# Windowed attention and a max-of-three FFN on one core: chunk 2's K and Q on GpSimd's queue, and a new order for the first five chunks

## The chip, the core and the metric

The kernel runs on one NeuronCore of a Trainium2 chip. A core has TensorE for matrix products (PE in the profile, its weight loads PEld), VectorE (DVE), ScalarE (ACT), GpSimd (POOL) and SyncE (SP), which here only starts transfers. GpSimd too starts transfers, on a queue of its own. Each engine works through its own instructions in program order and waits at each one until what it needs is there. The metric is the device time of one execution in microseconds, the median of several runs.

## The reference

Attention for 4 batches, 8 heads, 768 positions of 64 values: a query sees the 4 first keys of its batch (the sink) and the 128 latest keys up to itself. The result, 3072 tokens of 512 values, goes through an FFN with three weights of 512 x 768, of which the largest product is taken per element, and an output weight of 768 x 512.

```python
scores = scale * np.matmul(q, k.transpose(0, 1, 3, 2))
keep = is_sink | in_window              # pos < 4, or 0 <= rel < 128
a = softmax(np.where(keep, scores, -1e9))
x = np.matmul(a, v)                     # tokens x (heads * 64)
h = np.maximum(np.maximum(x @ w1, x @ w2), x @ w3)
return h @ w_out
```

All inputs and the output are float32; the kernel multiplies in bfloat16.

## The kernel before, in words

A chunk is 256 tokens of one batch with all 8 heads; there are 12, three per batch (`NCH`, `CPB`). Chunks 0 to 5 have one layout (`NEW = 6`), the later ones another. Heads go in four pairs p. Chunks 0, 3, 6 and 9 begin a batch and see no earlier keys.

The stages of a chunk ci, by helper:

- `load` (L93) starts a transfer of K, Q or V, whole (512 KB) or by halves of the heads (`part`), from SP's queue unless `eng` names another. A `gate` is a tiny GpSimd instruction that writes one element of the destination, so that the transfer waits for it: `pool_gate` (L605) waits for nothing but its place on GpSimd, `after(wi, c)` (L599) reads an element of FFN weight wi and so waits until the third of that weight with column c has landed. K, Q and V each have two buffers, so that chunk ci + 2 takes the one of chunk ci.
- `cast_qk` (L112) and `cast_v` (L121) turn float32 into bfloat16, a half of a chunk's Q or K, or a quarter of its V, on the engine that the call names.
- `turn` (L132), `turn2` (L156) and `turn_dma` (L177) transpose Q and K: the first two by TensorE with a copy from the accumulator memory (PSUM) by the engine named, the last by a transfer from SP.
- `premask` (L306) puts a pair's mask into its score banks ahead of the scores, by two matmuls of 512 columns (384 in a chunk that begins a batch). A pair without it is masked after the exponential by a VectorE multiply, `mask` (L401). `score` (L314) multiplies, `expo` (L392) takes the exponential on ScalarE, two instructions per pair.
- `sink_k` (L278), `sink_score` (L408) and `sink_v` (L431) do the four sink keys.
- `av_open` (L445) takes four PSUM banks, one per pair, and adds the sink's part; `av` (L460) multiplies a pair's weights by V, and VectorE divides by the sum: a reciprocal (L476) and a multiply (L479).
- `xpose` (L485) transposes the result x by TensorE, with two copies; `xpose_dma` (L496) by a transfer.
- `ffn_h` (L504): nine calls per chunk, third fp of the columns by weight wi, each of 8 matmuls with 256 columns (L517). The product with weight 0 is copied by ScalarE (L523), the others are merged by a maximum on VectorE (L527).
- `ffn_y` (L532): one of two halves of the tokens times the output weight, 6 matmuls of 512 columns (L540), and a copy. From chunk 3 on `y_turn` (L551, matmuls L564) does this. `store` (L591) writes a chunk's y from SP; `store_half` (L595) writes every second token row of it.

The weights come from GpSimd's queue, cast on the way: `load_w` (L289) nine times, a third of one weight each, and `load_wo` (L297) twice, half of the output weight.

PSUM has eight banks. `bank` hands out the one that has been free longest in the order of the program text, and `give` puts it back; so the text also sets which instruction waits for which bank.

The order of chunks 0 to 3, and of chunk 4 up to its FFN, is written out by hand, one helper call per line (L626 to L877). From L878 a loop handles iteration i: the attention of chunk i + 1, the FFN of chunk i, the output of chunk i - 1, the casts of chunk i + 2 on GpSimd and the loads of chunk i + 3. In the iterations i = 9 and i = 10 it also stores y of chunks 0 and 1 (one transfer of 1024 KB, both chunks lie in one tile) and of chunk 2.

In the written order, chunk 2's K (two halves) and Q (two halves) are started by SP (L697 to L704), gated by the second third of weight 0 and by GpSimd's place; chunk 2's V (L715) has the first gate too. GpSimd issues weight 2's thirds at L705 to L708, the output weight at L729. Chunk 1 has pairs 0 and 1 masked ahead of the scores and pairs 2 and 3 on VectorE; chunk 2 has all four on VectorE.

Of the kernel before, what the change touches and what calls it, by code (L numbers as in the profile page):

```python
# [16 lines left out]
def kernel(  # L17
# [31 lines left out]
    with tc.manual_schedule():  # L49
# [410 lines left out]
        def av(ci, p):  # L460
# [4 lines left out]
            for t in range(2):  # L465
                for a in range(2):
# [3 lines left out]
                    for s, cv, n in blocks:  # L470
# [3 lines left out]
                        first = False  # L474
            rc = work.tile([128, 2, 2], F32, tag="rc", bufs=4, name="rc")
# [9 lines left out]
        def xpose(ci, t, eng=None):  # L485
# [4 lines left out]
            for ds in range(DS):  # L490
                nc.tensor.transpose(
                    pt[:, ds], xs[ci][:, ds, t].rearrange("q a d -> q (a d)"), ident)
# [11 lines left out]
        def ffn_h(ci, fp, wi, cuts=1, eng=nc.scalar):  # L504
# [3 lines left out]
            for f in range(2):  # L508
                c0 = (2 * fp + f) * 128
                for ds in range(DS):  # L510
# [3 lines left out]
                    else:  # L514
# [5 lines left out]
                        start=(ds == 0), stop=(ds == DS - 1))  # L520
            dst = hs[ci][:, 2 * fp:2 * fp + 2]
# [103 lines left out]

        load(0, 'q', part=1, parts=2)  # L626
        warm(8)
        load(0, 'k')
        load(0, 'q', part=0, parts=2)
        load(0, 'v', part=0, parts=2, gate=pool_gate)  # L630
        cast_qk(0, 'q', 1, nc.scalar)
        load(0, 'v', part=1, parts=2)
        masks()
        sink_init()
        factors(msk, addm)
        turn(0, 'q', 1, nc.scalar)
        warm(4)
        premask(0, (2,))
        cast_qk(0, 'k', 0, nc.scalar)
        cast_qk(0, 'k', 1, nc.vector)  # L640
        turn(0, 'k', 1, nc.vector)
        load(1, 'k')
        turn(0, 'k', 0, nc.scalar)
        cast_qk(0, 'q', 0, nc.gpsimd)
        premask(0, (3,))
        score(0, (2,))
        score(0, (3,))
        turn(0, 'q', 0, nc.vector)
        premask(0, (0,))
        load(1, 'q')  # L650
        expo(0, 2)
        cast_v(0, 1, 0, nc.gpsimd)
        cast_v(0, 0, 0, nc.vector)
        cast_v(0, 1, 1, nc.vector)
        cast_v(0, 0, 1, nc.vector)
        load_w(0, 512, 768)
        load(1, 'v')
        score(0, (0,))
        expo(0, 3)
        cast_qk(1, 'k', 0, nc.gpsimd)  # L660
        premask(0, (1,))
        score(0, (1,))
        expo(0, 0)
        expo(0, 1)
        load_w(0, 256, 512)
# [3 lines left out]
        turn2(1, 'k', 0, nc.vector)  # L669
        cast_qk(1, 'k', 1, nc.scalar)  # L670
        av(0, 0)
        cast_qk(1, 'q', 0, nc.gpsimd)
        cast_qk(1, 'q', 1, nc.scalar)
        turn(1, 'k', 1, nc.scalar)
        load_w(0, 0, 256)
        av(0, 1)
        premask(1, (0,))
        turn2(1, 'q', 0, nc.vector)
        sink_k(0)
        premask(1, (1,))  # L680
        turn(1, 'q', 1, nc.scalar)
        cast_v(1, 0, 0, nc.vector)
        cast_v(1, 1, 0, nc.vector)
        load_w(1, 512, 768)
        xpose(0, 0, nc.vector)
        score(1, (0,))
        score(1, (1,))
# [190 lines left out]
        for i in range(4, NCH):  # L878
# [57 lines left out]
            if i == NCH - 2:  # L936
                store(2)
# [43 lines left out]
```

## Time and profile before

| what | us |
|---|---|
| three runs, median (lowest to highest) | 176.03 (175.41 to 176.61) |
| the profiled execution's own time | 175.3 |
| its span in the profile | 173.6 |
| TensorE busy | 167.1 |
| VectorE busy | 124.7 |
| GpSimd busy | 110.9 |
| ScalarE busy | 88.7 |

Times inside the profile count from the start of the span; 1.7 us of the profiled execution's time lie around it. "Busy" is the union of an engine's instruction times; TensorE's instructions overlap, so that it can count as busy while it delivers less than it could. The granted clock of TensorE was full throughout. A timeline row gives the start, the length, the engine, the line, the operation, its tile and shapes, how many, and in brackets how long the engine was idle before it and what ended that. A row of the chain of waits gives start, length, engine, tile, line and count. A row of stretches gives from:to, length, then busy time and number of instructions of TensorE, its weight loads, VectorE, ScalarE and GpSimd, the granted clock, the mean busy share of the DMA engines and GB/s. A row of one group of instructions gives the shortest, median and longest duration in ns.

### The profile page before, as it was taken

The page shows a single profiled execution, that of the slowest core. Times are in us where ns is not written, and L with a number is a line of the kernel's source. Part 1 is how long each engine was busy: PE and PEld are TensorE (multiplying, and loading weights), DVE is VectorE, ACT ScalarE, POOL GpSimd, SP SyncE. Part 2 cuts the span into 40 slices and gives each one's busy share as a digit, 9 for nine tenths or more (in the row PEclk, how much of TensorE's full clock was granted, in tenths as well). Part 3 has the DMA queues.
Part 4 walks back from the last instruction along what each step waited for, and adds up shares of the span by engine and source line. Part 5 has one row for each costly group of instructions (what it writes and reads, how often), then busy time and mean ns, then how long its engine had stood idle before and what let it go on. Part 6 is the DMA issues. An engine that isn't in the chain of part 4 may idle for free.

```text
span 173.6 us, 5416 instructions
## 1 busy us (share of the span) xinstructions
PE 167.1 (96%) x2225; PEld 128.6 (74%) x2225; DVE 124.7 (72%) x262; ACT 88.7 (51%) x183; POOL 110.9 (64%) x193
## 2 busy tenths in 40 slices
PE   7979999999999999999999999999999999999992
PEld 2546888857696697797797797797797896896871
DVE  3387854796797985986877976877777776776361
ACT  4778544677954614817726717717636516510210
POOL 7399507545499999999999999999998600000000
PEclk9999999999999999999999999999999999999999
DMA  4999999999999997988999999989999119017303
GB/s 139 301 288 198 218 217 256 221 306 276 280 195 216 190 273 124 245 199 216 253 199 252 195 224 246 265 168 227 264 195 259 32 33 377 21 34 272 121 2 121
DMA packets 71545, 35.22 MB, mean 203 GB/s; under 512 B 27488, under 2 KB 69984, under 8 KB 71520
## 3 DMA queue, kind: packets, MB, share of 16 engines
q1 hardware_dynamic: 65824, 31.60, 79.0%
q0 software_dynamic: 5552, 3.15, 12.7%
q8 instruction: 17, 0.28, 0.7%
q10 hardware_dynamic: 144, 0.13, 0.2%
q14 instruction: 8, 0.07, 0.1%
HBM read 25.17 MB, written 6.29 MB: 181 GB/s over the span
## 4 chain that ended last, share of the span: by engine, by line
PE 85%; DMA 7%; POOL 5%; issue 1%; DVE 0%; POOLq 0%; SPq 0%
PE h_ps L517 52%; PE y_ps L564 11%; PE y_ps L540 7%; PE o L471 6%; DMA w<-in_moe_w_dram 4%; PE st L357 3%; DMA v_raw<-in_v_dram 3%; PE st L331 2%; POOL w L292 2%; POOL vb L123 1%; PE pt L138 1%; PE o L453 1%; PE y_ps L586 1%; PE sk L423 1%; POOL q_bf L118 0%
## 5 line engine op out<-in xcount | busy, mean ns | idle before, releaser
L517 PE MATMUL h_ps<-xT,w 128*128 128x256 bf16 x864 | 101.2, 273 | 0.2 <-DMA w<-in_moe_w_dram 0.2
L517 PEld LDWEIGHTS <-w 128*128 128x128 bf16 x864 | 81.7, 98 | 10.7 <-issue 0.5
L527 DVE TENSOR_TENSOR h_sb<-h_sb,h_ps 128x512 bf16<-128x512 bf16 (+1 forms) x74 | 49.0, 670 | 17.4 <-PE h_ps L517 15.6
L523 ACT CAST h_sb<-h_ps 128x512 bf16<-128x512 f32 x35 | 20.6, 589 | 51.3 <-PE h_ps L517 51.2
L129 POOL CAST vb<-v_raw 32x512 bf16<-32x512 f32 x48 | 36.8, 766 | 2.5 <-DMA v_raw<-in_v_dram 0.3
L90 POOL CAST k_bf<-k_raw 32x512 bf16<-32x512 f32 x48 | 29.6, 616 | 2.2
L398 ACT ACTIVATE e_sb<-st 128x512 bf16<-128x512 f32 (+1 forms) x48 | 23.1, 583 | 1.1 <-PE st L331 1.1
L479 DVE TENSOR_TENSOR x_sb<-o,rc 128x256 bf16<-128x256 f32 x48 | 20.4, 424 | 1.7
L564 PE MATMUL y_ps<-wo,h_sb 64*64 64x512 bf16 (+1 forms) x312 | 21.1, 377 | 0.0
L471 PE MATMUL o<-vb,e_sb 128*128 128x65 bf16 x352 | 16.5, 193 | 0.8 <-DVE vb L123 0.8
L471 PEld LDWEIGHTS <-e_sb 128*128 128x128 bf16 x352 | 14.5, 97 | 3.1 <-ACT e_sb L398 1.0
L123 POOL CAST vb<-v_raw 64x512 bf16<-64x512 f32 x18 | 12.6, 697 | 5.7 <-DMA v_raw<-in_v_dram 5.1
L389 DVE TENSOR_TENSOR e_sb<-e_part,msk 128x1024 bf16<-128x1024 bf16 x16 | 13.1, 831 | 3.3 <-ACT e_part L374 3.1
L406 DVE TENSOR_TENSOR e_sb<-e_sb,msk 128x1024 bf16<-128x1024 bf16 (+1 forms) x18 | 13.6, 776 | 2.3 <-ACT e_sb L398 2.1
L564 PEld LDWEIGHTS <-h_sb 64*64 64x64 bf16 (+1 forms) x312 | 9.9, 106 | 5.0
L374 ACT ACTIVATE e_part<-st 128x384 bf16<-128x384 f32 x32 | 13.1, 495 | 0.5 <-PE st L357 0.5
L540 PE MATMUL y_ps<-wo,h_sb 128*128 128x512 bf16 x54 | 12.8, 380 | 0.0
L476 DVE RECIPROCAL rc<-o 128x4 f32<-128x4 f32 x48 | 8.4, 174 | 4.0 <-PE o L471 3.8
L118 POOL CAST k_bf<-k_raw 128x512 bf16<-128x512 f32 x6 | 3.8, 650 | 9.5 <-PE pt L138 6.8
L118 ACT CAST q_bf<-q_raw 128x512 bf16<-128x512 f32 x13 | 7.6, 620 | 3.0 <-DMA q_raw<-in_q_dram 3.0
L540 PEld LDWEIGHTS <-h_sb 128*128 128x128 bf16 x54 | 4.8, 98 | 5.4 <-DVE h_sb L527 0.8
L427 ACT ACTIVATE e_sink<-sk 128x256 bf16<-128x256 f32 x8 | 3.1, 389 | 10.0 <-PE sk L423 10.0
(90 smaller groups left out, 142.9 us busy)
## 6 DMA issues: line engine op xcount, KB each, us to landing
k_raw<-in_k_dram SPq DMA_DIRECT2D x11, 512.0 KB, 5.6
v_raw<-in_v_dram SPq DMA_DIRECT2D x11, 512.0 KB, 5.6
q_raw<-in_q_dram SPq DMA_DIRECT2D x10, 512.0 KB, 6.9
out_dram<-y_sb SPq DMA_DIRECT2D x9, 512.0 KB, 3.1
w<-in_moe_w_dram POOLq DMA_DIRECT2D x9, 256.0 KB, 6.1
q_raw<-in_q_dram SPq DMA_DIRECT2D x4, 256.0 KB, 7.6
out_dram<-y_sb SPq DMA_DIRECT2D x1, 1024.0 KB, 5.3
wo<-in_moe_w_out_dram POOLq DMA_DIRECT2D x2, 384.0 KB, 8.0
```

The lines of the kernel that those rows point to most:

```text
L90: f(bfs[ci, "k"][x:x + 32, :, n], raws[ci, "k"][y:y + 32, :, i].rearrange("q (p a) d -> q p a d", a=2))
L123: eng.tensor_copy(vb[ci % RING][64 * i:64 * i + 64, n, :, 0:D], raws[ci, "v"][64 * n:64 * n + 64, :, i])
L129: eng.tensor_copy(vb[ci % RING][x:x + 32, n, :, 0:D], raws[ci, "v"][y:y + 32, :, i])
L398: nc.scalar.activation(e[:, a, lo:], st[a][:, lo:], AF.Exp, scale=scale)
L406: (eng or nc.vector).tensor_mul(e[:, :, lo:], e[:, :, lo:], msk0[0] if lo else msk)
L471: nc.tensor.matmul(o[:, t, a], lhsT=e[:, a, s], rhs=vb[cv % RING][:, n, 2 * p + a], start=first, stop=True, skip_group_check=True)
L479: nc.vector.tensor_mul(xs[ci][:, p], o[:, :, :, 0:D], rc.unsqueeze(3).to_broadcast([128, 2, 2, D]))
L517: nc.tensor.matmul(hp[:, f].rearrange("q (i t r) -> q i t r", i=2, r=x.shape[3]), lhsT=w_sb[wi][:, ds, c0:c0 + 128], rhs=x, start=(ds == 0 ...
L523: (nc.scalar.copy if eng is nc.scalar else eng.tensor_copy)(dst, hp)
L527: nc.vector.tensor_max(dst[:, x], dst[:, x], hp[:, x])
L540: nc.tensor.matmul(yp, lhsT=hs[ci][:, fb, t * 128:(t + 1) * 128], rhs=wo[:, fb], start=(fb == 0), stop=(fb == FB - 1))
L564: nc.tensor.matmul(yps[ci][t][c:c + cols], lhsT=hs[ci][hp, fb, x:x + cols], rhs=wo[hp, fb], start=(turn == 0 and fb == 0), stop=(turn == 1 ...
```

## The change

Three helpers are split, so that the second half can stand elsewhere in the order: `av` and `norm` (the division), `ffn_h` and `ffn_max` (the copy or the maximum). `xpose` can take its four transposes in another order.

The written order of chunks 0 to 4 is new from end to end. What differs beside the order:

- Chunk 2's K and Q halves are issued by GpSimd, in its order between weight 1's last third and the end of weight 2: K, K, the first third of weight 2, Q, Q, the other two thirds. The output weight follows directly, where it came some ten calls later.
- Chunk 2's V waits for the last third of weight 2 (`after(2, 600)`) instead of weight 0's second. Chunk 4's Q comes ahead of chunk 3's V on SP's queue.
- Pair 3 of chunk 1 and pair 1 of chunk 2 are masked ahead of the scores, not on VectorE.
- Some casts and copies change engines: for instance chunk 0's first Q half goes to VectorE and chunk 5's Q from GpSimd to ScalarE and VectorE. One of chunk 5's V casts comes ahead of `masks2` on GpSimd.
- y of chunks 0, 1 and 2 is stored by halves, four and two transfers instead of one and one.

```diff
-        def av(ci, p):
+        def av(ci, p, then=True):
...
+            if then:
+                norm(ci, p)
+
+        def norm(ci, p):
+            o = os_[ci, p]
             rc = work.tile([128, 2, 2], F32, tag="rc", bufs=4, name="rc")
...
-        def xpose(ci, t, eng=None):
+        def xpose(ci, t, eng=None, order=range(DS)):
...
-            for ds in range(DS):
+            for ds in order:
...
-        def ffn_h(ci, fp, wi, cuts=1, eng=nc.scalar):
+        def ffn_h(ci, fp, wi, cuts=1, eng=nc.scalar, then=True):
...
+            maxima[ci, fp, wi] = hp
+            if then:
+                ffn_max(ci, fp, wi, cuts, eng)
+
+        def ffn_max(ci, fp, wi, cuts=1, eng=nc.scalar):
+            hp = maxima.pop((ci, fp, wi))
...
-                nc.sync.dma_start(
-                    out=out[0:512].rearrange("(c p i) d -> p c i d", c=2, i=2), in_=ys["01"])
+                for c in range(2):
+                    for x in range(2):
+                        store_half(c, x)
             if i == NCH - 2:
-                store(2)
+                for x in range(2):
+                    store_half(2, x)
```

The new order (the lines that the prediction follows, others left out):

```python
        sink_init()
        load(0, 'q', part=1, parts=2)
        cast_qk(0, 'q', 1, nc.vector)
        load(0, 'k')
        warm(8)
        cast_qk(0, 'k', 0, nc.scalar)
        load(0, 'q', part=0, parts=2)
        masks()
...
        cast_qk(0, 'k', 1, nc.gpsimd)
        turn(0, 'q', 1, nc.scalar)
        load(1, 'k')
        cast_qk(0, 'q', 0, nc.scalar)
        turn(0, 'k', 0, nc.scalar)
        turn(0, 'k', 1, nc.vector)
        premask(0, (3,))
        score(0, (2,))
        expo(0, 2)
...
        sink_k(0)
        load_w(0, 512, 768)
        cast_v(0, 0, 1, nc.vector)
        cast_qk(1, 'k', 0, nc.vector)
...
        expo(0, 1)
        av_open(0)
        av(0, 2)
        av(0, 3)
        load_w(0, 256, 512)
        cast_qk(1, 'k', 1, nc.scalar)
        load(1, 'q')
        cast_qk(1, 'q', 0, nc.gpsimd)
        load_w(0, 0, 256)
        turn2(1, 'k', 0, nc.scalar)
        premask(1, (1,))
        cast_qk(1, 'q', 1, nc.vector)
        turn(1, 'k', 1, nc.vector)
        av(0, 0)
        av(0, 1)
        premask(1, (0,))
        turn2(1, 'q', 0, nc.scalar)
        turn(1, 'q', 1, nc.vector)
        load_w(1, 512, 768)
        score(1, (1,))
        load_w(1, 256, 512)
        score(1, (0,))
        xpose(0, 0, nc.vector)
        xpose(0, 1, nc.vector)
        premask(1, (3,))
        expo(1, 1)
        load(1, 'v')
        cast_v(1, 0, 0, nc.gpsimd)
        cast_v(1, 1, 0, nc.vector)
        score(1, (3,))
        expo(1, 0)
        sink_v(0)
        cast_v(1, 1, 1, nc.vector)
        cast_v(1, 0, 1, nc.gpsimd)
        sink_score(1)
        expo(1, 3)
        load_w(1, 0, 256)
        load(2, 'k', part=0, parts=2, gate=after(0, 300), eng=nc.gpsimd)
        ffn_h(0, 2, 0, 1, nc.scalar)
        score(1, (2,))
        av_open(1)
        load(2, 'k', part=1, parts=2, eng=nc.gpsimd)
        load_w(2, 0, 256)
        load(2, 'q', part=1, parts=2, eng=nc.gpsimd)
        av(1, 0, then=False)
        av(1, 1, then=False)
        norm(1, 0)
        load(2, 'q', part=0, parts=2, gate=pool_gate, eng=nc.gpsimd)
        expo(1, 2)
        norm(1, 1)
        load_w(2, 256, 512)
        load_w(2, 512, 768)
        ffn_h(0, 1, 0)
        mask(1, 2)
        load_wo()
        av(1, 3, then=False)
        ffn_h(0, 0, 0)
        norm(1, 3)
        cast_qk(2, 'k', 0, nc.scalar)
        av(1, 2, then=False)
        cast_qk(2, 'k', 1, nc.gpsimd)
        ffn_h(0, 2, 1, then=False)
        norm(1, 2)
        xpose(1, 0, nc.vector, (0, 1, 3, 2))
        xpose(1, 1, nc.vector, (0, 1, 3, 2))
        ffn_h(0, 1, 1)
        load(2, 'v', gate=after(2, 600))
...
        load(3, 'q', gate=after(2, 300))
...
        premask(2, (1,))
...
        cast_v(2, 1, 0, nc.gpsimd)
...
        cast_v(2, 0, 0, nc.gpsimd)
        load(4, 'v')
        cast_v(2, 1, 1, nc.gpsimd)
        cast_v(2, 0, 1, nc.gpsimd)
        ffn_y(0, 0)
        ffn_y(1, 0)
        ffn_y(0, 1)
        av_open(2)
...
        av(2, 0)
        cast_qk(3, 'k', 1, nc.scalar)
        av(2, 1)
        av(2, 2)
        cast_qk(3, 'k', 0, nc.gpsimd)
        turn(3, 'k', 0, nc.scalar)
...
        cast_v(5, 0, 0, nc.gpsimd)
        load(6, 'v')
        load(6, 'q')
        masks2()
```

324 lines of the change are left out of this document (150 added, 174 removed).

## Prediction, blind

> **What bounds the kernel now.** I read the shares of busy time first, then the chain of waits, then the busy time of hand-chosen stretches, then the timeline of the first 23 us and of the stretch around 40 us, and last the transfers one by one.
>
> ```profile
> PE 167.1 (96%) x2225; PEld 128.6 (74%) x2225; DVE 124.7 (72%) x262; ACT 88.7 (51%) x183; POOL 110.9 (64%) x193
> ```
>
> ```profile
> 16.59 6.10 DMA w<-in_moe_w_dram
> 22.73 3.67 PE h_ps L517 x32
> ...
> 32.60 0.77 PE st L331 x18
> ...
> 36.87 2.70 PE y_ps L540 x12
> ...
> 40.04 0.48 PE o L471 x16
> ...
> 42.28 0.45 PE pt L138 x8
> ...
> 43.17 1.29 PE y_ps L540 x6
> ...
> 101.62 4.37 PE h_ps L517 x40
> ...
> 170.26 0.42 DVE y_sb L588
> ```
>
> ```profile
> 4.65:15.86 11.21, 9.49 (x128) 5.70 (x127) 7.51 (x20) 8.55 (x18) 8.12 (x13) 1.00 1.24 270
> 15.86:22.73 6.87, 6.71 (x94) 5.44 (x95) 5.28 (x14) 4.05 (x10) 3.97 (x9) 1.00 1.40 212
> 22.73:44.47 21.74, 21.74 (x238) 16.42 (x240) 14.46 (x30) 14.14 (x27) 10.34 (x19) 1.00 1.17 254
> ```
>
> The chain is TensorE without a break from 22.73 to 170.24; before 22.73 it is a weight transfer that lands at 16.59 + 6.10 = 22.69. So the time is: when the unbroken stretch begins, plus TensorE's work from there, plus the end. Only three things can move it: the 22.7 us ahead, TensorE work added or removed, and gaps hidden within the stretch.
>
> The chain gives TensorE's price per instruction: an FFN matmul 4.37/40 = 0.109, one of 512 columns 1.29/6 = 0.215, a transpose 0.45/8 = 0.056, a score 0.77/18 = 0.043, an attention-times-V one 0.48/16 = 0.03. By these prices 15.86 to 22.73 holds 40 FFN matmuls 4.37, 6 scores 0.26, 40 of the 0.03 kind 1.2 and 8 transposes 0.45: 6.28 of 6.87, so 0.6 lost. And 22.73 to 44.47 holds 104 FFN 11.36, 24 of y 5.16, 40 transposes 2.25, 24 scores 1.03, 40 at 0.03 1.2, the sink about 0.2: 21.2 of 21.74, so 0.5 lost. "Busy" hides this, since matmuls overlap. That is nearly all there is to win after 15.86; later loops are as dense as the row of 40.
>
> **The change, part by part.**
>
> *More TensorE work.* Pair 3 of chunk 1 and pair 1 of chunk 2 get their mask as two 512-column matmuls ahead of the scores in place of a VectorE multiply. Each pair adds 2 x 0.215 = 0.43 us to TensorE. The first falls into the slack ahead of 16 us (counted there). The second lies in the unbroken stretch: **+0.43**, in full. Bounds: 0.43 by the price above, 0.45 by the dearest 512-column row of the chain (2.70/12 each). The two multiplies that go (0.69 each, row 17.84 below) were beside TensorE.
>
> *The front, 0 to 22.7 us.*
>
> ```profile
> 5.75 0.62 ACT L118 CAST k_bf<-k_raw 128x512 bf16<-128x512 f32 x1
> ...
> 7.53 3.17 ACT L398 ACTIVATE e_sb<-st 128x384 bf16<-128x384 f32 x8
> ...
> 12.11 0.62 POOL L118 CAST q_bf<-q_raw 128x512 bf16<-128x512 f32 x1 [0.27 <-DMA q_raw<-in_q_dram]
> ...
> 12.87 0.42 DVE L479 TENSOR_TENSOR x_sb<-o,rc 128x256 bf16<-128x256 f32 x1
> ...
> 13.87 1.18 DVE L123 CAST vb<-v_raw 64x512 bf16<-64x512 f32 x2 [0.23 <-DMA v_raw<-in_v_dram]
> ...
> 14.42 2.06 ACT L398 ACTIVATE e_sb<-st 128x512 bf16<-128x512 f32 x4
> ...
> 14.98 0.73 DVE L493 COPY xT<-xt 128x512 bf16<-128x512 bf16 x2
> ...
> 17.84 0.69 DVE L406 TENSOR_TENSOR e_sb<-e_sb,msk 128x1024 bf16<-128x1024 bf16 x1 [0.22 <-ACT e_sb L398]
> ```
>
> I follow the new order on each engine with these durations. Chunk 0's second half of K lands at 5.75 as before. ScalarE then has a K cast, a Q copy, a Q cast and a K copy, four of some 0.6 less their overlap, before the first exponential: 8.05 in place of 7.53; eight of them take 3.17, to 11.2. Its cast of K1 ends at 11.85, and TensorE transposes that before it multiplies pairs 0 and 1 of chunk 0 (about 12.6). VectorE meanwhile waits for Q1, which lands at 12.1 (row 12.11), casts it (0.43), copies a K transpose (0.42) and only then normalises the two pairs (2 x 0.55): x is whole at 14.1, where before it was at 12.87 + 0.42 = 13.29. But before, 1.18 of V casts then stood ahead of the xT copies; now they stand behind them. With the Q copy and two xT copies of 0.42, xT is whole at 15.7, as before (14.98 + 0.73). TensorE has the extra mask, a score and the sink's two small steps in front of its first FFN matmuls: **16.1 against 15.86** (where I cut the stretches above). From there the same 6.28 of work, with two short waits that I see: the attention banks of chunk 1 open when pair 3's exponentials are half done (ScalarE 14.35 + 2.06 + 0.4 + 0.53 = 17.4, 0.1 lost), and pair 2 is the one pair still masked on VectorE (its exponentials end at 19.55, plus 0.69: 0.3 lost). So 16.1 + 6.28 + 0.4 = **22.8 for what is done at 22.73 now: +0.1**, its mask matmuls included. Bounds: 21.7, if the stretch ran unbroken from the landing of the first weights (below), and 23.8, if one more hand-over of some 1 us comes in.
>
> *Chunk 2's K and Q, output weight, V2.*
>
> ```profile
> L292 POOL DMA_DIRECT2D w<-in_moe_w_dram x1: 1105/1105/1105, 9.4 to 9.4; - x1
> ...
> DMA to landing us min/median/max: 5.5/5.5/5.5
> ```
>
> ```profile
> L292 POOL DMA_DIRECT2D w<-in_moe_w_dram x2: 771/776/782, 13.8 to 14.6; - x2
> ...
> DMA to landing us min/median/max: 5.8/6.0/6.2
> ```
>
> ```profile
> L292 POOL DMA_DIRECT2D w<-in_moe_w_dram x2: 750/756/762, 18.3 to 19.0; - x2
> ...
> DMA to landing us min/median/max: 9.7/10.5/11.4
> ```
>
> ```profile
> L107 SPq DMA_DIRECT2D v_raw<-in_v_dram x1: 2047/2047/2047, 20.5 to 20.5; - x1
> ...
> DMA to landing us min/median/max: 11.6/11.6/11.6
> ```
>
> ```profile
> 32.30 1.27 POOL L123 CAST vb<-v_raw 64x512 bf16<-64x512 f32 x2 [2.16 <-DMA v_raw<-in_v_dram]
> ...
> 39.40 0.41 PE L471 MATMUL o<-vb,e_sb 128*128 128x65 bf16 x8
> ...
> 40.44 0.62 POOL L118 CAST k_bf<-k_raw 128x512 bf16<-128x512 f32 x1 [1.13 <-DMA k_raw<-in_k_dram]
> ```
>
> The first weight third is issued some 0.5 later (the sink's copies now stand ahead of it on GpSimd): 9.4 + 5.5 + 0.5 = 15.4, ahead of 16.1, no cost. GpSimd then issues four loads more, unknown in price there: 0.75 each as a weight third, up to 1.1 (the row at 9.4): 3.0 to 4.4 us. It has the room (3.97 busy of 6.87). I take 0.75, as the load is cut into as many pieces; the last third of weight 2 is then issued at 22.5, at the worst 25.3, both ahead of its turn on the wire. On the wire a weight third alone takes 20.8 - 19.6 = 1.2 (rows at 13.8 and 14.6), half a chunk's Q 0.88 (Q1 lands at 12.1, V1 at 13.87). After weight 1's last (about 22.0) come four halves and three thirds, 3.5 + 3.6: the last lands at 29.1. With the price of a mixed pair, 30.4 - 28.0 = 2.4 (landings of the rows at 18.3 and 19.0), it is 30.1. I take 29.5, since SP's queue is now empty there. TensorE's first need of each piece is later by 1 us or more, so no wait.
>
> What is new: GpSimd waits for that landing before it releases V2, then Q3 and K3. V2 leaves SP at 29.6 in place of 20.5. Behind the gate on GpSimd stand only casts that need the same loads. Pairs of chunk 2 are multiplied after three y groups instead of two, so at 39.4 + 1.3 = 40.7; four V2 casts take 2 x 1.27: V2 must land by 38.1. I expect 29.6 + 1.76 + the output weight on the other queue (3 thirds, 3.6) = 35.0. K3 landed at 40.4; now the same bytes end at 38.4 to 40.4, and its cast (0.62) is wanted at 41.5. No cost in the sum, slack 3.1 and 0.4 to 2.4. The output weight is issued 4 us sooner; half a y group waits for it now (2.70 against 2 x 1.29): -0.1, within the 0.5.
>
> The Trainium skill ("DMA: Bandwidth & Descriptors", section "Issuing engines are not separate DMA queues") says that it matters little which engine starts a transfer, as all share 16 DMA engines. By that the move saves nothing on the wire, the last third lands at 30.4 as now, K3 0.9 later than I take it, and the sum would be about 0.5 higher; by the rows of single transfers it is as above. The mixed pair's 2.4 against 1.2 + 0.88 speaks a little against the rule.
>
> *From 22.8 on.* The work 21.2 + 0.43 without a wait that I can find gives 44.4 against 44.47: the lost 0.5 goes, the extra mask eats it.
>
> *Later.* Chunks 3 and 4 hold the same work in another order; the one wait there now (0.42 for chunk 3's transposed x) stays. The rows are of the timeline, of the chain (chunk 8's first scores) and of two single transfers:
>
> ```profile
> 53.67 0.31 POOL L241 MEMSET keep<- 128x256 bf16 x1
> ...
> 58.26 1.64 PEld L517 LDWEIGHTS <-w 128*128 128x128 bf16 x16 [0.42 <-DMA xT<-x_sb]
> ...
> 155.61 5.24 SPq L592 DMA_DIRECT2D out_dram<-y_sb  x3
> ```
>
> ```profile
> 106.21 0.46 PE st L357 x24
> ```
>
> ```profile
> L107 SPq DMA_DIRECT2D v_raw<-in_v_dram x1: 526/526/526, 51.1 to 51.1; - x1
> ...
> DMA to landing us min/median/max: 4.1/4.1/4.1
> ```
>
> ```profile
> L188 SPq DMA_TRANSPOSE kT<-k_bf x1: 4704/4704/4704, 95.4 to 95.4; - x1
> ...
> DMA to landing us min/median/max: 8.9/8.9/8.9
> ```
>
> The halved stores (four and two issues for one and one) lie on SP behind the transposes and 14 us ahead of the end at 170.26 + 0.42; the three stores there take 5.24. Zero; without that cover one more issue, about 1 us or less.
>
> *Sum.* +0.1 front, +0.43 mask, -0.5 gaps: 0.0. The profiled execution took 175.3 (span 173.6), 0.7 under the median of 176.03; the same from the median: **176.0**.
>
> **Rivals.**
>
> *Slower: the gate on weight 2.* One mechanism: V2 and K3 are released too late. V2 took 11.6 from issue now, with K2 and Q2 ahead of it in its own queue. At 11.6 again: 41.2 + 2.5 of casts = 43.7, TensorE waits 3.0: 179.0. It decides from a V2 landing after 38.1 (8.5 us from issue), or a K3 after 40.8. For it: every wait of TensorE is paid in full. Against it: the queue ahead is empty. About 178 if half comes true.
>
> *Slower by less: GpSimd falls behind.* A V5 cast now stands ahead of the late masks on GpSimd. These begin at 53.67 now; V5 lands at 51.1 + 4.1 = 55.2, so some 1.5 us of delay, which the casts of all later chunks inherit. Chunk 8's K transpose, issued at 95.4, lands 8.9 later at 104.3, its first scores are at 106.21: the slack is 1.9, so it costs only beyond that: 176 to 177.
>
> *Faster: the front closes up.* From the weights at 15.4, 6.28 without a gap is 21.7: -1.05; with -0.5 of gaps, -0.4 of the xT wait, +0.43: -1.5, 174.5. More than about -1.7 isn't there to be had.
>
> *No effect:* the queues' new order is hidden anyway; the same time as the forecast.
>
> **How the numbers follow.** Forecast (no effect among it) 0.54, own range 175.1 to 177.0; gate 0.21; GpSimd 0.08; front 0.17. The range leaves out half of the front's deeper end and the gate's upper end: 174.0 to 178.4. One per cent, about what a measurement can tell, is 174.27 and 177.79: faster 0.14, same 0.62, slower 0.24.
>
> **What would show it.** First FFN matmuls near 16.1 and chunk 1's transposes near 21.5; weight 2 landing near 29.5; V2 casts on GpSimd from about 35; an unbroken TensorE chain with first chunk-3 scores near 44.4. Wrong would be: waits of TensorE for V2, K3 or the output weight between 35 and 43, or FFN matmuls from 15 on with no gaps.

## The result and the profile after

| kernel | median, us | lowest to highest | runs |
|---|---|---|---|
| before | 175.94 | 175.40 to 177.38 | 22 |
| after | 176.82 | 176.24 to 178.17 | 22 |

The ratio is 1.0047, 95% interval 1.0030 to 1.0063: slower by 0.9 us, half a per cent. That is within the one per cent and within the range of the prediction, but clear of zero, and zero is what its sum gave. The profiled execution of after took 176.56 (span 174.8), 0.3 under its median; that of before took 175.3, 0.6 under its median. The spans differ by 1.2, the medians by 0.9.

The first line is from the page of after (busy time of each engine), the next ones from its view of stretches, cut at the same work as those of before: first FFN matmul, the fifth FFN call and chunk 1's transposes done, first scores of chunk 3, and as a new mark the sink scores of chunk 5.

```profile
PE 168.0 (96%) x2229; PEld 129.4 (74%) x2229; DVE 126.9 (73%) x263; ACT 87.8 (50%) x182; POOL 113.1 (65%) x195
```

```profile
4.65:16.23 11.58, 10.11 (x129) 5.73 (x127) 7.88 (x23) 8.59 (x19) 8.85 (x14) 1.00 1.25 265
16.23:22.68 6.45, 6.45 (x98) 5.54 (x95) 4.78 (x14) 4.24 (x9) 5.82 (x11) 1.00 1.36 230
22.68:44.90 22.22, 22.22 (x240) 16.66 (x239) 14.81 (x28) 13.22 (x26) 10.72 (x20) 1.00 1.16 262
44.90:68.70 23.80, 23.11 (x274) 18.26 (x272) 20.00 (x43) 11.90 (x26) 18.26 (x37) 1.00 0.87 189
```

And the last stretch of before:

```profile
44.40:67.52 23.12, 23.12 (x273) 17.97 (x272) 19.30 (x42) 11.53 (x24) 19.81 (x39) 1.00 1.10 218
```

So the profiled executions differ like this: the front is 0.05 shorter (22.68 against 22.73), the stretch to chunk 3's first scores 0.55 longer (22.22 against 21.67, by the rows at 44.40), the stretch to chunk 5's sink scores 0.68 longer (23.80 against 23.12), and from there to the end both take 106.1. From the first FFN matmul on, the last row of after is the only one of after in which TensorE is busy for less than the stretch: 0.69 idle. The timeline shows where. Rows of TensorE, its weight loads, VectorE and GpSimd in after:

```profile
45.88 2.78 PE L524 MATMUL h_ps<-xT,w 128*128 128x256 bf16 x24
...
46.23 0.61 POOL L118 CAST k_bf<-k_raw 128x512 bf16<-128x512 f32 x1
46.91 1.57 POOL L123 CAST vb<-v_raw 64x512 bf16<-64x512 f32 x2
...
47.18 0.83 DVE L118 CAST q_bf<-q_raw 128x512 bf16<-128x512 f32 x1
47.93 0.83 DVE L118 CAST k_bf<-k_raw 128x512 bf16<-128x512 f32 x1
48.68 1.02 DVE L406 TENSOR_TENSOR e_sb<-e_sb,msk 128x768 bf16<-128x768 bf16 x2
...
49.28 0.54 PE L471 MATMUL o<-vb,e_sb 128*128 128x65 bf16 x12 [0.62 <-POOL ks L283]
...
49.28 0.42 PEld L471 LDWEIGHTS <-e_sb 128*128 128x128 bf16 x12 [0.90 <-DVE e_sb L406]
...
53.84 0.42 DVE L118 CAST q_bf<-q_raw 128x512 bf16<-128x512 f32 x1
```

The same place in before, with the rows up to chunk 3's FFN:

```profile
46.25 2.79 PE L517 MATMUL h_ps<-xT,w 128*128 128x256 bf16 x24
48.88 0.53 PE L471 MATMUL o<-vb,e_sb 128*128 128x65 bf16 x12
...
54.91 1.47 PE L540 MATMUL y_ps<-wo,h_sb 128*128 128x512 bf16 x6
56.32 0.61 PE L331 MATMUL st<-qT,kT 64*128 64x128 bf16 x12
56.86 1.47 PE L540 MATMUL y_ps<-wo,h_sb 128*128 128x512 bf16 x6
```

In before the 24 FFN matmuls start at 46.25 and chunk 3's first attention product follows 2.63 later, before their modelled end. In after it follows 3.40 later: 0.77 lost. The two rows at 49.28 name different releasers, the matmul GpSimd's sink copy, the weight load VectorE's mask. The attention product reads what VectorE masked and not the sink's keys, and a_m30 below settles it: VectorE (in a_mask21, with the same wait, the matmul's row names the mask too). The mask of chunk 3's pair 0 stands at 48.68 behind two casts for chunk 4, which take 0.83 each; the same cast takes 0.42 at 53.84, when GpSimd is not casting.

### The profile page after: what moved, and what is told of

Its sections match the earlier page's. It is cut to its first block, busy times and chain, and to the rows that moved or that the text cites. A ratio compares the mean times of both kernels' runs of the same rounds, so it can differ in the third digit from the quotient of the medians.

```text
span 174.8 us, 5427 instructions
## 1 busy us (share of the span) xinstructions
PE 168.0 (96%) x2229; PEld 129.4 (74%) x2229; DVE 126.9 (73%) x263; ACT 87.8 (50%) x182; POOL 113.1 (65%) x195
## 4 chain that ended last, share of the span: by engine, by line
PE 70%; DMA 15%; POOL 10%; issue 2%; SPq 1%; DVE 0%; POOLq 0%
PE h_ps L524 44%; PE y_ps L577 11%; PE o L471 5%; DMA w<-in_moe_w_dram 4%; DMA q_raw<-in_q_dram 4%; PE y_ps L553 4%; POOL vb L123 4%; DMA k_raw<-in_k_dram 4%; PE st L357 3%; DMA v_raw<-in_v_dram 3%; POOL w L292 2%; PE st L331 1%; POOL q_raw L107 1%; SPq L107 1%; PE o L453 1%
## 5 line engine op out<-in xcount | busy, mean ns | idle before, releaser
L536 ACT CAST h_sb<-h_ps 128x512 bf16<-128x512 f32 x36 | 21.1, 592 | 46.5 <-PE h_ps L524 45.5
L129 POOL CAST vb<-v_raw 32x512 bf16<-32x512 f32 x48 | 34.6, 721 | 2.3
L90 POOL CAST k_bf<-k_raw 32x512 bf16<-32x512 f32 x48 | 31.6, 658 | 2.2
L398 ACT ACTIVATE e_sb<-st 128x512 bf16<-128x512 f32 (+1 forms) x48 | 23.3, 583 | 2.3 <-PE st L331 2.3
L406 DVE TENSOR_TENSOR e_sb<-e_sb,msk 128x1024 bf16<-128x1024 bf16 (+1 forms) x16 | 13.0, 836 | 2.9 <-ACT e_sb L398 2.9
L118 ACT CAST q_bf<-q_raw 128x512 bf16<-128x512 f32 x14 | 8.2, 622 | 0.0
L331 PE MATMUL st<-qT,kT 64*128 64x128 bf16 (+1 forms) x128 | 7.3, 238 | 0.6 <-ACT qT L168 0.5
```

The source lines that it names most:

```text
L90: f(bfs[ci, "k"][x:x + 32, :, n], raws[ci, "k"][y:y + 32, :, i].rearrange("q (p a) d -> q p a d", a=2))
L129: eng.tensor_copy(vb[ci % RING][x:x + 32, n, :, 0:D], raws[ci, "v"][y:y + 32, :, i])
L398: nc.scalar.activation(e[:, a, lo:], st[a][:, lo:], AF.Exp, scale=scale)
L536: (nc.scalar.copy if eng is nc.scalar else eng.tensor_copy)(dst, hp)
```

## The experiments

Eighteen runs. In all of them the whole computation is done. Each kernel is timed beside before on the same chip; a ratio is to that, and 0.1% is 0.18 us. To see what happens inside, the profile of each is cut at the marks above: "front" is the time at which the fifth FFN call and chunk 1's transposes are done (in the new order the first FFN matmul behind the transposes plus 8 of 0.109), then the stretch to chunk 3's first scores, the stretch to chunk 5's sink scores, and the rest of the span. The marks are starts of TensorE rows in each timeline.

| kernel | median, us | ratio and interval | front | to chunk 3 | to chunk 5 | rest |
|---|---|---|---|---|---|---|
| before, profile | 175.94 | | 22.73 | 21.67 | 23.12 | 106.1 |
| after | 176.82 | 1.0047 (1.0030 to 1.0063) | 22.68 | 22.22 | 23.80 | 106.1 |
| b_pm21 | 176.50 | 1.0043 (1.0015 to 1.0071) | 22.61 | 22.77 | 23.21 | 106.0 |
| b_queue | 176.52 | 1.0037 (1.0012 to 1.0062) | 22.53 | 22.25 | 23.55 | 106.4 |
| b_transfers | 176.84 | 1.0050 (1.0022 to 1.0078) | 22.46 | 22.97 | 23.24 | 106.3 |
| b_halves | 176.13 | 1.0006 (0.9985 to 1.0028) | 23.59 | 21.60 | 23.22 | 106.4 |
| b_v5 | 175.82 | 0.9985 (0.9959 to 1.0011) | 23.04 | 21.60 | 23.25 | 106.0 |
| a_mask21 | 176.87 | 1.0055 (1.0034 to 1.0076) | 22.93 | 21.82 | 23.83 | 106.1 |
| a_gate | 176.90 | 1.0045 (1.0021 to 1.0069) | 22.88 | 22.22 | 24.06 | 106.1 |
| a_sp | 181.48 | 1.0282 (1.0241 to 1.0323) | 23.41 | 25.04 | 23.24 | 106.4 |
| a_m30 | 176.86 | 1.0051 (1.0032 to 1.0071) | 22.76 | 22.22 | 24.15 | 106.1 |
| a_both | 176.58 | 1.0039 (1.0013 to 1.0065) | 22.99 | 21.79 | 24.51 | 106.1 |
| a_x3 | 176.56 | 1.0036 (1.0013 to 1.0060) | 22.83 | 22.22 | 23.96 | 106.1 |
| a_x3v | 177.31 | 1.0061 (1.0030 to 1.0092) | 23.20 | 22.23 | 23.00 | 106.9 |
| a_x3v21 | 177.57 | 1.0082 (1.0055 to 1.0109) | 22.78 | 21.82 | 23.70 | 107.6 |
| a_x3vk | 177.73 | 1.0091 (1.0058 to 1.0123) | 23.00 | 22.22 | 23.46 | 106.8 |
| a_x3vk21 | 177.88 | 1.0084 (1.0054 to 1.0113) | 23.14 | 21.96 | 23.40 | 107.1 |
| h_ab | 176.39 | 1.0032 (1.0012 to 1.0051) | 22.60 | 22.22 | 23.35 | 106.1 |
| h_ab21 | 176.02 | 1.0021 (0.9995 to 1.0047) | 23.30 | 21.79 | 23.31 | 106.1 |
| h_ba | 177.28 | 1.0092 (1.0060 to 1.0124) | 23.67 | 21.93 | 24.32 | 106.4 |

The front differs by some 0.5 either way between profiles of equal fronts (22.6 to 23.7 in the old order): the first FFN matmuls start sooner or later (16.15 to 16.86 in the new order), and the old order waits for weight 1's last third for anything from nothing to 0.81. The three columns behind it hardly move unless a wait does.

### Single parts of the change, made in the kernel before

**b_pm21**, the mask matmuls of chunk 2 pair 1 alone:

```diff
+        premask(2, (1,))
         score(2, (1,))
...
-        mask(2, 1)
```

> The kernel before with one part of the change: pair 1 of chunk 2 masked ahead of its scores by two 512-column matmuls, VectorE's multiply taken out. Theory 'more TensorE work': 0.43 us more, about 176.4 against 175.95. Rival 'VectorE needed the relief': VectorE, which is 90 per cent busy in that stretch, comes free sooner and the time stays the same or falls.

Plus 0.7 in the medians. The timeline of b_pm21 shows the matmuls between the scores, where nothing hides them:

```profile
32.88 0.62 PE L331 MATMUL st<-qT,kT 64*128 64x128 bf16 x12
33.42 0.61 PE L311 MATMUL st<-addm,ident 128*128 128x512 bf16 x2
33.96 0.40 PE L331 MATMUL st<-qT,kT 64*128 64x128 bf16 x6
```

From 33.42 to 33.96 they take 0.54 here. A wait for a Q cast comes on top, 0.25, and one for chunk 1's transposed x, 0.27, so that the stretch is 1.1 longer. VectorE, which the expectation calls 90 per cent busy, is busy for 14.46 of the 21.74 us of that stretch in before.

**b_queue**, chunk 2's K and Q on GpSimd's queue among weight 2's thirds, and **b_transfers**, which adds V2's late gate and the early output weight:

```diff
-        load(2, 'k', part=0, parts=2, gate=after(0, 300))
+        load(2, 'k', part=0, parts=2, gate=after(0, 300), eng=nc.gpsimd)
...
-        load(2, 'v', gate=after(0, 300))
...
+        load(2, 'v', gate=after(2, 600))
```

> The kernel before with one part of the change: chunk 2's K and Q halves issued by GpSimd, in the changed kernel's order among the thirds of weight 2. V2 keeps its place on SP and its early gate. Theory 'hidden': TensorE waits for none of these pieces, 0.0, at most 0.2 either way. Rival 'the queue costs': GpSimd's four added issues and the later thirds of weight 2 make TensorE wait for a weight or for Q of chunk 2 between 26 and 32 us: 0.3 to 1.5 more.

> The kernel before with the whole change to the early transfers: chunk 2's K and Q on GpSimd's queue, V2 released only when the last third of weight 2 has landed, the output weight issued right after weight 2. The order of the computing is left as it was. Theory 'hidden': within 0.2 of the kernel before, or 0.1 less, since half a y group no longer waits for the output weight. Rival 'the gate': V2 lands some 4 us later than now (32.1), and in this order chunk 2's first attention-times-V product stands at 39.4, so with casts of 2.5 it starts to wait when V2 lands after 36.9: 0 to 2 us more.

Both miss: plus 0.6 and 0.9. In b_queue's profile TensorE no longer waits for weight 1's last third (front 22.5), but neither does it in b_pm21, whose transfers are those of before; and in both the 32 FFN matmuls behind chunk 1's transposed x take longer to the next start (3.78 and 3.77, in before 3.50). So these two differences can't be put down to the queue. What b_queue has beyond that is a wait for a cast of chunk 3's Q (0.86 from 39.87 to 40.73, in before 0.48 from 39.88 to 40.36) and a longer one at chunk 3's FFN (1.82 from 57.25 to 59.07, in before 1.40 from 56.86 to 58.26):

```profile
40.73 0.40 PE L138 MATMUL pt<-ident,q_bf 128*128 128x128 bf16 x4 [0.21 <-DVE q_bf L118]
...
59.07 1.92 PE L517 MATMUL h_ps<-xT,w 128*128 128x256 bf16 x16 [0.35 <-DMA xT<-x_sb]
```

In b_transfers V2 lands at 35.3, in before at 32.1. GpSimd's casts then run beside VectorE's masks of chunk 2; three of these take 3.94 in place of 2.30 (the first row is of before, the others of b_transfers), and TensorE waits for one, 0.83:

```profile
36.96 2.30 DVE L406 TENSOR_TENSOR e_sb<-e_sb,msk 128x1024 bf16<-128x1024 bf16 x3
```

```profile
36.90 3.94 DVE L406 TENSOR_TENSOR e_sb<-e_sb,msk 128x1024 bf16<-128x1024 bf16 x3
...
40.89 0.66 PE L471 MATMUL o<-vb,e_sb 128*128 128x65 bf16 x16 [0.83 <-DVE e_sb L406]
```

**b_halves**, the stores alone:

```diff
-                store(2)
+                for x in range(2):
+                    store_half(2, x)
```

> The kernel before with one part of the change: y of chunks 0 to 2 stored by halves. Theory 'covered': 0.0. Rival 'the stores cost': more and smaller pieces near the end delay the last transposed x or the last stores: 0.2 or more.

Nothing, as forecast.

### Parts of the change undone in the kernel after

**a_mask21** (pair 1 of chunk 2 masked on VectorE again), **a_gate** (V2's old gate), **a_sp** (K2, Q2 and V2 as in before, on SP's queue):

```diff
-        premask(2, (1,))
...
+        mask(2, 1)
```

```diff
-        load(2, 'v', gate=after(2, 600))
+        load(2, 'v', gate=after(0, 300))
```

```diff
-        load(2, 'q', part=1, parts=2, eng=nc.gpsimd)
+        load(2, 'q', part=1, parts=2)
```

> The changed kernel, with pair 1 of chunk 2 masked by VectorE again instead of by two 512-column matmuls. Theory 'more TensorE work': those two matmuls lie in TensorE's unbroken stretch and cost 0.43 us in full, so 0.4 us less than the changed kernel (about 176.4 against 176.8), 0.4 above the kernel before. Rival 'VectorE needed the relief': the fourth multiply of some 0.9 us makes VectorE late for the attention-times-V products of chunk 2, a wait takes the place of the matmuls and the time stays at 176.8 or rises.

> The changed kernel with one gate put back: chunk 2's V waits for weight 0's second third, as before, not for weight 2's last. K2, Q2 stay on GpSimd's queue. Theory of the gates (mask of chunk 3 pair 0, then chunk 3's transposed x, then chunk 5's K transpose stand in a chain, and each takes what the one ahead gives up): V2 leaves SP some 4 us sooner and Q3, K3 behind it too, but chunk 3's scores are bound by TensorE, so 176.6 to 176.9, nothing gained. Rival (the late transfers are the cost, since they push the loads of chunks 3 to 5 back): minus 0.4 to 0.9, 176.0 to 176.4.

> The changed kernel with all of chunk 2's loads put back on SP: K and Q halves by SP's queue at their new places in the order, V with the gate on weight 0's second third. GpSimd then issues four loads fewer, some 3 us of its time between 17 and 24 us. Theory of the gates: the same moves cost 0.9 us when made alone in the kernel before, but in the new order they only shift which wait ends last: 176.5 to 176.9. Rival (the transfers are the cost in either order): minus 0.9, near 175.9.

a_mask21 gains its 0.40 in the stretch to chunk 3 (21.82 against 22.22) and gives nothing back behind it; its profiled execution had a front 0.25 later, and the medians show no gain. So its price stands in the profile, and the median, whose interval is 0.4 wide to either side, doesn't confirm it. a_gate changes nothing that its interval (0.4 to either side) could show: in the new order the late release of V2 has no price. a_sp is the surprise: 4.7 us slower than after by the medians, 4.1 by the ratios to before, which no theory had. Its profiled execution took 179.76, the least of its six, and holds 3.3 of that (span 178.1 against 174.8), 2.8 of it in the stretch to chunk 3. There TensorE waits for chunk 2's last Q half:

```profile
29.75 0.39 PE L138 MATMUL pt<-ident,q_bf 128*128 128x128 bf16 x4
32.79 0.40 PE L138 MATMUL pt<-ident,q_bf 128*128 128x128 bf16 x4 [2.65 <-ACT q_bf L118]
```

The two Q halves one by one (issue, and time from issue to landing), a_sp and then after:

```profile
L107 SPq DMA_DIRECT2D q_raw<-in_q_dram x2: 555/895/1235, 18.4 to 19.1; - x2
...
DMA to landing us min/median/max: 10.4/11.7/13.0
```

```profile
L107 POOL DMA_DIRECT2D q_raw<-in_q_dram x2: 752/762/772, 19.9 to 21.0; - x2
...
DMA to landing us min/median/max: 6.5/6.7/6.8
```

On SP they leave 1.5 to 1.9 us sooner and land 2 to 4 us later. GpSimd, which has four loads fewer, then issues weight 2 and the output weight early on the other queue (the output weight's first half at 19.5, in after at 23.3), and all share the wire; on one queue Q2 comes in its turn ahead of the output weight. In before, on SP as well, the two halves took 10.4 and 11.4 us, so the last landed at 30.6, and were transposed at 30.24 and 31.34. The new order transposes both at 29.02. So it loses by SP's queue in two ways, which no run separates: it wants Q2 sooner, and Q2 lands later with the early output weight under way (that this is why is argued, not shown).

The Trainium skill ("DMA: Bandwidth & Descriptors", section "Issuing engines are not separate DMA queues") says that the engine which starts a transfer matters only for the time it takes to start it, since all run on the same 16 DMA engines. They do share them here: between 14 and 40 us of a_sp the packets of GpSimd's queue took 78.6% of the 16 engines' time and those of SP's 48.3%, which is more than all of it. But with the other queue the halves took 10.4 and 13.0 us from issue to landing in place of 6.5 and 6.8, so more than the time to start a transfer hung on the choice here.

### Waits moved out of the way

**a_m30**, the mask of chunk 3 pair 0 ahead of chunk 4's casts, and **a_both**, which takes a_mask21 in as well:

```diff
         expo(3, 0)
+        mask(3, 0)
         cast_qk(4, 'q', 1, nc.vector)
```

> The changed kernel, with chunk 3's mask of pair 0 moved on VectorE ahead of chunk 4's casts of Q and K (no work added or left out). Theory 'late mask': TensorE's gap ahead of chunk 3's first attention-times-V product (48.5 to 49.3) ends with that mask, which stands behind two casts of 0.83 us; without them the gap shrinks to 0.1 or less and the time falls by 0.6 to 0.7, to about 176.1. Rival 'late V': the gap ends with GpSimd's last V cast or sink copy of that chunk (48.5 to 49.3), which the edit does not move; then the time stays at 176.8 and the gap stays.

> The changed kernel with both edits: VectorE's mask for pair 1 of chunk 2, and chunk 3's mask of pair 0 ahead of chunk 4's casts. If the two costs are separate they add: 1.0 to 1.1 us less than the changed kernel, 175.7 to 175.8, which is 0.2 to 0.3 under the kernel before. Rival 'the queues cost something too': it stays above the kernel before.

The wait at chunk 3's attention is gone, as the rows of a_m30 show, and a longer one stands at chunk 3's first FFN matmul:

```profile
48.48 0.60 POOL L283 COPY ks<-kT 64x16 bf16<-64x16 bf16 x2
48.57 0.53 PE L471 MATMUL o<-vb,e_sb 128*128 128x65 bf16 x12
...
59.86 1.21 PEld L524 LDWEIGHTS <-w 128*128 128x128 bf16 x12 [1.16 <-DMA xT<-x_sb]
```

The attention product now starts while GpSimd's sink copy still runs, so that copy was not what it waited for in after. It follows the 24 FFN matmuls by 2.62, as in before, so 0.77 is won; 1.0 is lost again to the transfer that transposes chunk 3's x, and the median stays. a_both misses too (176.58, expected 175.7 to 175.8): it has the same wait for that transfer, and its stretch to chunk 5 gives back 0.36 of the 0.43 that the mask saves.

**a_x3** adds an earlier division of chunk 3's last pair to a_m30, so that its x is transposed sooner; **a_x3v** also holds the load of V5 back behind that transpose, **a_x3v21** takes a_mask21 in; **b_v5** holds V5 back in before:

```diff
-        ffn_h(2, 0, 2)
-        cast_qk(5, 'q', 1, nc.vector)
-        load(5, 'v', gate=pool_gate)
+        ffn_h(2, 0, 2, then=False)
         av(3, 2)
+        ffn_max(2, 0, 2)
+        cast_qk(5, 'q', 1, nc.vector)
         xpose_dma(3)
+        load(5, 'v', gate=pool_gate)
```

> The changed kernel with chunk 3's x finished sooner on VectorE: the mask of pair 0 ahead of chunk 4's casts, and the division of pair 2 ahead of the maximum of (2, 0, 2) and of the cast of chunk 5's Q. Theory 'x of chunk 3': the time from 59 us on is set by the landing of its transposed x; its transfer then leaves 1.0 to 1.5 us sooner than in the changed kernel (54.87), and the time falls by 0.4 to 0.8, to 176.0 to 176.4. If chunk 5's V, which leaves SP just ahead, makes the transfer longer (5.4 in place of 4.5 us), most of it is lost again: 0 to 0.3. Rival 'TensorE's work': nothing but the extra mask matmuls counts, 0.0.

> As the run with chunk 3's x finished sooner, and chunk 5's V load put behind the transfer of that x on SP (its cast on GpSimd behind the late masks, as in the kernel before). Theory 'x of chunk 3': the transfer no longer shares the wire with V5, takes 3.4 to 4.0 us, and TensorE does not wait for it: 0.8 to 1.2 under the changed kernel, 175.6 to 176.0. Rival 'V5 is no part of it': the same time as without moving V5.

> As the run before it (x of chunk 3 sooner, V5 behind it), and pair 1 of chunk 2 masked by VectorE. If the transposed x no longer holds TensorE, the 0.43 us of mask matmuls that got lost in the wait before now show: 0.3 to 0.45 under the run with V5 moved, 175.2 to 175.6, under the kernel before. If VectorE then ends the wait, 0.0.

> The kernel before with chunk 5's V load put behind the transfer of chunk 3's x on SP, nothing else. Theory 'x of chunk 3': the transfer takes 3.4 to 4.0 us in place of 4.8 to 5.3, the wait of 0.4 at 58.3 goes: 0.2 to 0.4 less than the kernel before. Rival 'V5 is no part of it': 0.0.

In a_x3 the weight load's wait for the transposed x is down from 1.16 to 0.53, and the median is 0.3 under after, the upper end of what was expected if V5 makes the transfer longer (it took 5.7 us). In a_x3v the stretch to chunk 5 is 23.00, shorter than in before, and no row of TensorE's matmuls in it names a wait. But SP's queue now has V5 and three loads ahead of chunk 5's transposes, and the scores of chunk 5 wait; the "rest" grows by 0.8, in a_x3v21 by 1.5. So both miss, by more than 1 us. b_v5 is the same as before within its interval.

**a_x3vk** and **a_x3vk21** put chunk 5's transposes ahead of those loads:

```diff
         xpose_dma(3)
+        turn_dma(5, 'k')
+        turn_dma(5, 'q')
+        load(6, 'q')
+        load(6, 'k')
         load(5, 'v', gate=pool_gate)
+        load(6, 'v')
```

> The kernel a_x3v with chunk 5's K and Q transposes issued right behind chunk 3's x on SP, ahead of the loads of Q6, K6, V5 and V6. a_x3v took 177.31 with a wait of 0.6 us for chunk 5's transposed K at the scores of chunk 5. Theory of the gates: that wait goes, near 176.6, unless a fourth one stands right behind (the casts of chunk 6 on GpSimd, whose loads leave later now). Rival (the cost lies in TensorE's own work, the waits only show it): 177.3 again.

> a_x3vk with chunk 2 pair 1 masked on VectorE again, so that TensorE has 0.43 us less. Here all the gates that the earlier runs showed are moved out of the way and the added TensorE work of the unbroken stretch is gone as well. a_x3v21 took 177.57 with a wait of 1.5 for chunk 5's K. Theory of the gates: minus 1.5, near 176.1, 0.4 to 0.5 below a_x3vk. Rival: as a_x3v21, 177.6, or no gap to a_x3vk since a further wait takes it.

That wait goes too. VectorE's maxima now cost 0.2 near chunk 3's attention (23.46), and the next whole wait stands 13 us later, at chunk 6's scores; the medians, 177.7 and 177.9, are no lower than in a_x3v. The weight-load rows of a_x3v and of a_x3vk:

```profile
69.58 0.23 PEld L331 LDWEIGHTS <-kT 64*128 64x128 bf16 x8 [0.82 <-DMA kT<-k_bf]
```

```profile
82.46 0.31 PEld L357 LDWEIGHTS <-kT 64*64 64x64 bf16 x16 [0.98 <-DMA kT<-k_bf]
```

So four gates stand one behind another: VectorE's mask of chunk 3, chunk 3's transposed x, chunk 5's K, chunk 6's K. Each one that is moved lets the next take 0.6 to 1.0.

### The two halves of the new order, each with the other half of the old

**h_ab** has the new order up to chunk 2's transposed x and the old one from there to the loop; **h_ba** the other way about; **h_ab21** is h_ab with a_mask21's edit.

```diff
         xpose(2, 1, nc.vector)
-        load(5, 'k', gate=after(0, 300))
-        score(3, (1,))
-        expo(3, 1)
...
+        load(5, 'k', gate=after(0, 300))
+        cast_qk(4, 'q', 1, nc.vector)
+        score(3, (1,))
```

> The changed order up to the transposes of chunk 2's x, the order of before from there to the loop (first scores of chunk 3 to chunk 4's x). It holds the mask matmuls of chunk 2 pair 1 and all of the new transfers, but not the new order of chunks 3 and 4. Theory (0.43 for the mask matmuls up to chunk 3's first scores, and the rest, some 0.4, at chunk 3's attention, where the mask of its pair 0 stands behind two casts of chunk 4): the second term goes, 176.3 to 176.5 beside 176.0 of before. Rival (the new front with its transfers costs all of it): 176.8 to 176.9. Second rival (the later order is all that costs): 176.0.

> The other way about: the order of before up to the transposes of chunk 2's x, the changed order from there to the loop. No mask matmuls added, the transfers as before. Theory: the later term alone, plus 0.3 to 0.5, 176.3 to 176.5. Rival (the front costs all): 176.0. Second rival (the later order is all): 176.8.

> h_ab with chunk 2 pair 1 masked on VectorE again. Theory: both terms are gone, 175.9 to 176.1, so 0.4 below h_ab. If a wait behind takes the 0.43 again, as it did in the changed kernel, it equals h_ab.

h_ab came out a little above the theory (plus 0.7, expected 0.3 to 0.5, after 0.9), h_ab21 on it (0.4 below h_ab, 0.3 above before, an interval that holds zero). h_ba missed: plus 1.6. The halves don't add up: 0.7 and 1.6 against 0.9 together. The new later order behind old arrivals waits twice, 0.45 for the mask and 0.46 at chunk 3's FFN; the profiled execution (178.01, 0.7 above the median) also waits 0.81 for weight 1's last third. In the profile the old later order saves 0.45 (23.35 against 23.80); the medians give 0.2 to 0.4, which the intervals don't tell from nothing.

No kernel here is measurably faster than before.

## Why the prediction was wrong, point by point

- *More TensorE work, +0.43.* Right: 0.40 to 0.43 in four of the five pairs of profiles in the new order that differ in it alone (22.22 against 21.79 in h_ab and h_ab21, 21.82 in a_mask21); in the fifth, a_x3vk21, a wait takes 0.2 of it. In the old order the two matmuls took 0.54 (b_pm21). The medians of the same five pairs differ by 0.3 to 0.4 in two (a_both, h_ab21) and show no gain in three (a_mask21, a_x3v21, a_x3vk21); their intervals are about as wide.
- *The front, 22.8 for what is done at 22.73.* Right for these profiles: 22.68, first FFN matmuls at 16.23 (forecast 16.1), with 0.17 lost behind them where it expected 0.4. What it left out: the profile of before waited 0.17 for weight 1's last third, while the old front waited 0.58 in b_halves, 0.81 in h_ba and 0.42 in b_v5, as its row shows:

```profile
23.04 2.14 PE L517 MATMUL h_ps<-xT,w 128*128 128x256 bf16 x18 [0.42 <-DMA w<-in_moe_w_dram]
```

  The new front never waits there. Five profiles with the old front end it at 22.6 to 23.7, 23.1 in the mean, twelve with the new one (all but a_sp) at 22.6 to 23.3, 22.9 in the mean. That is very likely why the medians differ by 0.9 and the two profiles by 1.2; it was not tested by itself.
- *Transfers, no cost in the sum.* Right in the new order. Weight 2's last third landed at 29.98 (forecast 29.5), V2 left at 30.31 and landed at 35.68 (35.0), and GpSimd cast it without TensorE waiting. Rows of the chain of waits of after:

```profile
22.52 7.46 DMA w<-in_moe_w_dram
...
30.31 5.37 DMA v_raw<-in_v_dram
```

  a_gate shows that the rival "gate on weight 2" had no part. That the moves would be free in any order was not said, and is not so: b_transfers.
- *From 22.8 on: "the lost 0.5 goes, the extra mask eats it".* **This step failed.** Forecast for the stretch was 21.6, measured 22.22. Without the mask matmuls it is 21.8, against 21.67 and 21.60 in the old order: the 0.5 was still lost. Behind the start at 22.73 no row of TensorE's matmuls in the stretch names a wait, in before or after. Of the weight loads two in before name one, 0.17 for a K cast at 27.39 and 0.42 for a copy of xT at 44.40, behind the six y matmuls counted below. The 0.5 was the difference between a count of matmuls times their price and the clock, and I took what the count left over for gaps. From one start to the next, most of it lies where TensorE goes over to scores. Rows of before, then of after:

```profile
31.56 1.04 PE L517 MATMUL h_ps<-xT,w 128*128 128x256 bf16 x8
32.53 0.84 PE L331 MATMUL st<-qT,kT 64*128 64x128 bf16 x18
...
33.53 2.79 PE L517 MATMUL h_ps<-xT,w 128*128 128x256 bf16 x24
36.25 0.40 PE L331 MATMUL st<-qT,kT 64*128 64x128 bf16 x6
```

```profile
30.57 1.04 PE L524 MATMUL h_ps<-xT,w 128*128 128x256 bf16 x8
31.54 0.84 PE L331 MATMUL st<-qT,kT 64*128 64x128 bf16 x18
...
32.75 2.78 PE L524 MATMUL h_ps<-xT,w 128*128 128x256 bf16 x24
35.46 0.29 PE L423 MATMUL sk<-qT,ks 128*32 128x256 bf16 x4
```

  The 8 and the 24 FFN matmuls take 0.97 and 2.72 in before, each 0.10 more than 0.109 apiece, and 0.97 and 2.71 in after, where the second group stands ahead of the sink's scores. Six y matmuls ahead of scores (43.01 to 44.40 in before) take 0.10 more than their price, and six scores 0.07. That is 0.37 of the 0.5, and the new order pays it likewise. The weight loads there sit idle for 0.16 to 0.42, mostly with "issue" named, which means nothing that the profile shows; what TensorE does in that time stays open.
- *Later: "the same work in another order; the one wait there now (0.42) stays".* **Failed too**, by 0.68 in the profile. The 0.42 for chunk 3's transposed x in before was no loss: the six y matmuls ahead of it take 1.40 to the next start (56.86 to 58.26) and the six before those 1.41 (54.91 to 56.32), where no transfer is waited for. Behind those, before's weight loads show the same 0.42 with no releaser:

```profile
56.31 0.39 PEld L331 LDWEIGHTS <-kT 64*128 64x128 bf16 x12 [0.42 <-issue]
```

  And the new order has a true wait, 0.77 at chunk 3's attention, since the prediction did not follow VectorE's queue past chunk 2: the two casts of chunk 4 ahead of that mask, 0.83 each, stand in none of its sums, and the one Q cast on VectorE that it prices has 0.43. Where this wait is gone and at most 0.2 of another stands in its place, the stretch is 23.24 (a_sp) and 23.00 (a_x3v), against 23.12 in before. After has its twelve y matmuls in one piece, 2.69 (56.20 to 58.89): one change of kind fewer gives 0.1 back.
- *Stores by halves, zero.* Right (b_halves).
- *GpSimd behind* had no part: the rest is 106.1 in both. *The front closes up* came partly, as the weight wait that is gone.

So the mechanism forecast for the front and the price of the mask were right, but the sum held a gain of 0.5 that was never there and lacked a wait of 0.77. The front of a usual run of before, later than the one profiled, very likely hid a part of that, so that the time still fell within the range; that part is luck.

What stays open: how far the medians' 0.9 goes to the later order (0.2 to 0.4 by h_ab) rather than to the mask and the rest of the front, since the intervals are about as wide as these terms.

## What to carry to other kernels

A difference between counted work and the clock is no gap to win until a row names what ended it; look whether the same small idle time stands where nothing could be waited for. In an order that is tuned end to end, judge an edit by marks inside the profile, not by the end alone: the next wait takes what the edit gives, here four times running. And before a transfer is called free, ask whose turn on the wire it takes, and what will run beside the casts that it sets off: with chunk 2's loads on GpSimd's queue one order was 0.6 to 0.9 us slower, and the other more than 4 faster.

## What the runs showed of the hardware

- A VectorE cast of 128x512 from float32 to bfloat16 took 0.42 us alone and 0.83 where a cast of GpSimd's had started ahead of it; two of GpSimd's took 1.57 there, where one takes 0.61 (rows of after above). Where VectorE's started first, it kept its time and GpSimd's took 0.84. Rows of before:

```profile
45.59 0.43 DVE L118 CAST k_bf<-k_raw 128x512 bf16<-128x512 f32 x1 [0.83 <-DMA k_raw<-in_k_dram]
45.65 0.84 POOL L118 CAST k_bf<-k_raw 128x512 bf16<-128x512 f32 x1 [1.49 <-DMA k_raw<-in_k_dram]
```

  The Trainium skill ("SBUF — State Buffer", section "SBUF: two separate sides") says that the two engines share a pair of ports under an exclusive lock and that the loser blocks for a whole instruction. The trace agrees in the main: the one that starts later is the longer one. One VectorE cast that started 0.25 us before a GpSimd cast ended took 0.43 all the same (43.91 in before).
- The transfer that transposes a chunk's x took 4.5 us in after, 5.4 in a_m30 and 3.1 in a_x3v, where V5's load was held back behind it. Rows of a_m30 and of a_x3v:

```profile
L503 SPq DMA_TRANSPOSE xT<-x_sb x1: 1244/1244/1244, 54.4 to 54.4; - x1
...
DMA to landing us min/median/max: 5.4/5.4/5.4
```

```profile
L503 SPq DMA_TRANSPOSE xT<-x_sb x1: 1233/1233/1233, 53.8 to 53.8; - x1
...
DMA to landing us min/median/max: 3.1/3.1/3.1
```

  In b_v5, a_x3vk and a_x3vk21, with V5 behind it too, it still took 5.0, 4.6 and 4.9, so a load ahead is not all that sets it.
